# One load of five weight rows issued as five strided loads, and two small loads issued by ScalarE, in a gated attention decode step

## The chip, the cores and the metric

The kernel runs on one core of a Trainium2 chip. A core has five engines, each with its own instruction stream: TensorE (PE) multiplies matrices, VectorE (DVE) and GpSimd (POOL) do elementwise work and reductions, ScalarE (ACT) does activations and copies, and SyncE (SP) mostly issues DMAs. Sixteen DMA engines move data between the chip's main memory (HBM) and the core's on-chip memory (SBUF), which has 128 partitions. The metric is the time of one execution on the device, in microseconds (us).

## The reference

The step mixes one token's attention over a cache with a feed-forward layer, by a gate:

```
def _A_ref(x, k_cache, v_cache, wq, wo):          # B=2, Sq=1, D=640, H=32, Sk=4096, Dh=128
    q = (x @ wq).reshape(B, Sq, H, Dh).transpose(0, 2, 1, 3)
    scores = einsum("bhqd,bhkd->bhqk", q, k_cache) * (Dh ** -0.5)
    o = einsum("bhqk,bhkd->bhqd", softmax(scores), v_cache)
    return o.transpose(0, 2, 1, 3).reshape(B, Sq, H * Dh) @ wo
def _B_ref(x, w1, w2):                            # w1: 640 x 1728, w2: 1728 x 640
    return silu(x @ w1) @ w2
g = sigmoid((x * gate_w).sum(-1, keepdims=True))
return g * _A_ref(...) + (1 - g) * _B_ref(...)
```

Everything is float32. The two caches hold 134 MB each, the weights some 30 MB, and each byte of them is used once.

## The kernel before

SBUF holds three slabs of 64 KB per partition, `v`, `b` and `a` (`slabs`). The work runs through stages:

- **Start.** SP loads w1 into slab `a`, then x and the gate vector into the small tile `xs` (4 to 8 partitions of 640 bytes each), then w2 and wq. `xs` is cleared by POOL first (line 332), so x waits for that clear. DVE transposes `xs` (line 449), takes gate products (lines 453 to 460) and multiplies w1 by x (lines 472 and 475); PE finishes the feed-forward part (lines 487 and 567) and makes the queries (line 642). ACT's first instruction loads an activation table; its first work is the gate's exponential (line 506).
- **Sixteen items**, each a group of four heads for one of the two batch entries. For an item a K slab of 8.4 MB and a V slab of 8.4 MB are loaded. POOL and DVE multiply K by the query (lines 707 and 713), DVE sums and finds the peak (lines 723 to 741), ACT takes exponentials (line 752), PE multiplies by V (line 799), and DVE and PE fold the result into the columns `oP` (lines 821 to 871). K alternates between slabs `a` and `b`, V uses `v` and at the last item `a`.
- **End.** The 4096 rows of wo come in four groups (`load_wo`): two of them as one load of 5.1 MB and one as a load of 2.6 MB, into slab `v`, and the last one into slab `b`, cut in three: five of the eight rows that a partition holds (12,800 bytes in each of 128 partitions), then two rows (5,120 bytes), then one (2,560 bytes). PE multiplies the first three groups at line 590 (`in_halves`), ACT copies the sum at line 602, PE folds it at line 607 (`merge`), and the last group is multiplied at line 620 (`in_quarters`), which waits for the five rows, then for the two, then for the one. DVE copies the result (line 929) and SP stores it.

Every load is issued by SP, in program order, from one line (72, `Flow.dma`). `Flow` records operations with what they read and write; `plan` gives each its waits on semaphores. A load counts its own semaphore up by 16 when all of it has landed. The loads of wo are issued as soon as the last K slab and the last but one V slab have been used, and queue behind the last V load. A load of 128 partitions is served by all sixteen DMA engines; each engine has its own queue of the packets that are its share.

```
        cuts = (0, PD) if g < NP - 1 else (0, FIRST * D, PD - D, PD)
        after = f.users(part(n)) if g == NP - 1 else v_users
        for k, (c0, c1) in enumerate(zip(cuts, cuts[1:])):
            f.dma("SP", slab[n][:, at + c0 : at + c1], src[:, c0:c1], writes=part(n, g % (NP - 1) + k), after=after)
```

Of the kernel before, what the change touches and what calls it, by code (L numbers as in the profile page):

```python
# [189 lines left out]
def gated_decode(nc, x, kc, vc, wq, wo, w1, w2, gate, out):  # L190
    P = 128
# [4 lines left out]
    Q = 4  # L196
# [10 lines left out]
    HB = 16  # L207
# [4 lines left out]
    NP = HQ // 2  # L212
# [8 lines left out]
    f = Flow(nc)  # L221
    V, S_, T_, G_ = nc.vector, nc.scalar, nc.tensor, nc.gpsimd

    def sb(name, shape, align=32):
        return nc.alloc_sbuf_tensor(name, shape, F32, align_bytes=align)[tuple([slice(None)] * len(shape))]
# [7 lines left out]
    slab = {n: slabs[:, k * SLAB : (k + 1) * SLAB] for k, n in enumerate("vba")}  # L233

    def part(n, *ks):
        return [f"{n}.{k}" for k in (ks or range(8))]
# [13 lines left out]
    g = sb("g", [P, NP * B])  # L250
# [19 lines left out]
    oP, xs = oP_xs[:, : -D // Q], oP_xs[:, -D // Q :]  # L270
# [5 lines left out]
    oT = ps_m[:64, 256:512].rearrange("p (n r) -> p n r", r=32)  # L276
    early, acc = ps_acc[:, :W2], ps_0[:, :W]

    h_e, h_v, h_o, *h_k = (f.sem(n) for n in ("weights", "values", "rows", "even", "odd"))


# [32 lines left out]
    def load_wo(g):  # L314

        n, at = ("v", g * PD) if g < NP - 1 else ("b", 0)
        if g == 0:
            src = wo[: 2 * PR * P, :].rearrange("(g p n) d -> p g (n d)", g=2, n=PR)
            to = slab["v"][:, : 2 * PD].rearrange("p (g c) -> p g c", g=2)
            f.dma("SP", to, src, writes=part("v", 0, 1), after=v_users)  # L320
            return
        if g == 1:
            return
        src = wo[g * PR * P : (g + 1) * PR * P, :].rearrange("(p n) d -> p (n d)", n=PR)
        cuts = (0, PD) if g < NP - 1 else (0, FIRST * D, PD - D, PD)
        after = f.users(part(n)) if g == NP - 1 else v_users
        for k, (c0, c1) in enumerate(zip(cuts, cuts[1:])):
            f.dma("SP", slab[n][:, at + c0 : at + c1], src[:, c0:c1], writes=part(n, g % (NP - 1) + k), after=after)

    f.op("POOL", lambda: G_.memset(oP_xs, 0.0), writes=["oP", "xs"])
    f.dma("SP", slab["a"][:, : J * F], w1.rearrange("(p j) f -> p (j f)", j=J), writes=part("a"))
    f.dma("SP", xs[0:P:HB, :], x.rearrange("b s (c n) -> (s c) b n", c=Q), reads=["xs"], writes=["xs0"])
    f.dma("SP", xs[HB // 2 : P : 32, :], gate.rearrange("(c n) -> c n", c=Q), reads=["xs"], writes=["xs1"])
    f.dma(
        "SP",
        slab["v"][:, : FH * HD],
# [1 line left out]
        writes=part("v", 0),  # L340
# [9 lines left out]
        reads=["ident"],  # L350
        writes=["ident"],
# [11 lines left out]
        reads=["ident"],  # L363
        writes=["block"],
# [6 lines left out]
        reads=["block"],  # L371
        writes=["fold"],
# [4 lines left out]
        reads=["ident"],  # L377
        writes=["sel"],
# [4 lines left out]
        reads=["ident"],  # L383
        writes=["half"],
# [9 lines left out]
        reads=["sel"],  # L394
        writes=["pick"],
# [4 lines left out]
        reads=["sel"],  # L400
        writes=["own"],
# [4 lines left out]
        reads=["ident"],  # L406
        writes=["side"],
# [6 lines left out]
        reads=["block"],  # L414
        writes=["spread"],
# [4 lines left out]
        reads=["ident"],  # L420
        writes=["mask"],
    )
    f.op("DVE", lambda: V.memset(join, 0.0), writes=["join"])
    for e in range(2):
        ends, at = join[:, e, ::HB], 64 + HB * (1 - e)
# [5 lines left out]
            reads=["ident", "join"],  # L431
            writes=["join"],
        )
        for t in (at, at + 32):
# [3 lines left out]
                reads=["ident", "join"],  # L438
                writes=["join"],
# [10 lines left out]
        reads=["xs0", "xs1"],  # L450
        writes=["xt"],
# [5 lines left out]
        reads=["xt"],  # L457
        writes=["gx"],
    )
    f.op("DVE", lambda: V.reduce_sum(gp, gx.rearrange("p j b -> p b j"), axis=AX.X), reads=["gx"], writes=["gp"])  # L460
    rows = ps_v
# [4 lines left out]
    for b in range(B):  # L466
        for j in range(J):
            at = xt[:, j, HB * b : HB * b + 1]
# [11 lines left out]
                reads=part("a") + ["xt"],  # L480
                writes=[f"hsum{b}"],
            )

    def mm_hr():
# [18 lines left out]
        reads=["ones", "gp"],  # L503
        writes=["ps_o"],
# [6 lines left out]
        reads=["ge"],  # L511
        writes=["g"],
# [4 lines left out]
        reads=["g"],  # L517
        writes=["gc"],
# [7 lines left out]
    for e in range(2):  # L526
# [3 lines left out]
            reads=["ps_v"],  # L530
            writes=[f"spaced{e}"],
# [8 lines left out]
        reads=["he", "gc"],  # L540
        writes=["he"],
    )
    for e in range(2):
# [5 lines left out]
            reads=["he", "turned", "half", "seq"],  # L549
            writes=[f"seq{e}"],  # L550
# [125 lines left out]
    for u in range(2):  # L676
        for b in range(B):
# [7 lines left out]
                reads=[f"ps_{u}", "mask"],  # L685
                writes=[f"qall{u}{b}"],
# [200 lines left out]
    for i in range(N + 1):  # L887
# [21 lines left out]
        if i == N - 1:  # L909
            v_users = f.users(part("v"))  # L910
            for g_ in range(NP):
                load_wo(g_)
# [45 lines left out]
    ops, at = f.ops["PE"], 0  # L958
    while at < len(ops):
# [7 lines left out]
        at = end  # L967
# [21 lines left out]
```

## Time and profile before

| | us |
|---|---|
| median of three runs | 696.17 (695.96 to 696.38) |
| the profiled execution's own time | 695.97 |
| its span, first to last instruction | 694.6 |

| engine | busy in the span, us | share |
|---|---|---|
| DVE | 506.9 | 73% |
| POOL | 265.6 | 38% |
| PE | 211.9 | 31% |
| ACT | 40.0 | 6% |

No compute engine is near full. The page of the profile cuts the span into 40 slices; in its row "DMA" a 9 says that the sixteen DMA engines were busy 90% of the slice or more. The same quantity can be asked for any stretch: a row of the table of windows gives the stretch and its length, then the busy time of each engine in it with the number of instructions, the granted TensorE clock, the mean busy share of the DMA engines, and the rate in GB/s. A packet is counted in the window in which it starts, so that short windows are grainy. In the timeline a row gives start, duration, engine, line, operation, output and inputs, and in brackets how long the engine had been idle and what ended that; "SPq" is SP's sequencer issuing a DMA. A row of the DMA issues gives the number of loads, the size of one, and the time from issue to landing.

### The profile page before, as it was taken

How to read it: one execution, taken by the hardware profiler on the slowest of the kernel's cores; microseconds unless marked ns; L12 is line 12 of the kernel's file. 1: busy time of each engine (PE TensorE's matmuls, PEld its weight loads, DVE VectorE, ACT ScalarE, POOL GpSimd, SP SyncE). 2: the span in 40 equal slices, each digit the busy share in tenths (PEclk: the TensorE clock that was granted, in tenths of full speed). 3: DMA queues.
4: the chain of work that ended last, by engine and by line, in shares of the span. 5: the costliest groups of instructions: out<-in, count | busy, mean ns of one | idle time of the engine just before them, and what ended most of it. 6: DMA issues, size and time to landing. Idle time of an engine off the chain costs nothing. (4 is left out here: it accounts for less than half of the span.)

```text
span 694.6 us, 3767 instructions
## 1 busy us (share of the span) xinstructions
PE 211.9 (31%) x1440; PEld 70.2 (10%) x1440; DVE 506.9 (73%) x269; ACT 40.0 (6%) x152; POOL 265.6 (38%) x26
## 2 busy tenths in 40 slices
PE   0073033151331506060412305060513215060556
PEld 0031010010110101010100101010101001010112
DVE  3910958898989697886959596986959595977901
ACT  0001010101010101010010101010000101010100
POOL 1000908190827090815335180906244270907100
PEclk9997556565565657566575757575665757575779
DMA  9999999999999999999999999999999999999997
GB/s 383 429 426 473 426 423 427 423 464 434 423 430 423 442 457 423 423 430 434 464 423 423 430 426 468 426 423 430 423 468 430 423 430 423 453 445 423 430 417 309
DMA packets 6051, 298.32 MB, mean 429 GB/s; under 512 B 652, under 2 KB 672, under 8 KB 928
## 3 DMA queue, kind: packets, MB, share of 16 engines
q1 hardware_dynamic: 6048, 298.27, 99.3%
q8 instruction: 3, 0.05, 0.0%
HBM read 298.26 MB, written 0.01 MB: 429 GB/s over the span
## 5 line engine op out<-in xcount | busy, mean ns | idle before, releaser
L707 POOL TENSOR_TENSOR slabs<-slabs,qsb 128x7680 f32<-128x7680 f32 x16 | 262.4, 16400 | 378.9 <-DMA slabs<-in_A_k_cache_dram 330.8
L723 DVE TENSOR_REDUCE s<-slabs 128x68 f32<-128x8704 f32 (+1 forms) x32 | 276.3, 8677 | 0.0
L799 PE MATMUL ps<-slabs,pz 128*32 128x512 f32 x1024 | 147.2, 739 | 337.1 <-PEq L156 328.9
L713 DVE TENSOR_TENSOR slabs<-slabs,ps 128x8704 f32<-128x8704 f32 x16 | 147.5, 9221 | 103.8 <-DMA slabs<-in_A_k_cache_dram 103.2
L799 PEld LDWEIGHTS ps<-slabs,pz 128*32 128x32 f32 x1024 | 39.7, 132 | 433.5 <-issue 425.2
L752 ACT ACTIVATE pz<-s,nb 32x128 f32<-32x128 f32 x64 | 25.5, 398 | 545.8 <-PE ps L799 353.2
L837 PE MATMUL ps<-osb,pick 128*128 128x512 f32 x32 | 21.1, 747 | 60.9 <-PEq L156 59.9
L821 DVE SCALAR_TENSOR_TENSOR osb<-ps,rg,own 128x512 f32<-128x512 f32 x16 | 12.0, 750 | 23.4 <-PE ps L799 23.1
L852 DVE TENSOR_REDUCE row<-ps 64x128 f32<-64x512 f32 x16 | 10.9, 682 | 24.0 <-PE ps L837 24.0
L773 PE MATMUL ps<-rs,fold 128*128 128x1 f32 x32 | 6.2, 262 | 40.9 <-PEq L156 40.8
L475 DVE SCALAR_TENSOR_TENSOR slabs<-slabs 128x1728 f32<-128x1728 f32 x8 | 16.2, 2019 | 0.3
L487 PE MATMUL ps<-slabs,xz_col 128*32 128x432 f32 x16 | 3.1, 927 | 33.4 <-DVE slabs L475 33.4
L837 PEld LDWEIGHTS ps<-osb,pick 128*128 128x128 f32 x32 | 5.4, 211 | 75.0 <-issue 73.1
L752 ACT ACTIVATION_READ_ACCUMULATOR pz<-s,nb 32x1 f32 x64 | 11.8, 184 | 0.0
L773 PEld LDWEIGHTS ps<-rs,fold 128*128 128x128 f32 x32 | 6.2, 226 | 54.2 <-issue 53.3
L859 DVE STREAM_TRANSPOSE ps<-row 64x256 f32<-64x256 f32 x16 | 10.3, 643 | 0.6
L567 PE MATMUL ps<-slabs,seq 128*32 128x320 f32 x54 | 9.2, 496 | 3.7 <-DVE seq L546 3.7
L642 PE MATMUL ps<-slabs,xz_col 128*32 128x512 f32 x80 | 9.8, 593 | 0.0
L652 PE MATMUL ps<-qall,spread 128*128 (+1 forms) x32 | 9.0, 371 | 0.8 <-ACT qall L680 0.8
L929 DVE COPY slabs<-ps 128x160 f32<-128x160 f32 x1 | 0.3, 324 | 11.9 <-PE ps L620 11.9
L590 PE MATMUL ps<-slabs,oP_xs 128*32 128x320 f32 x96 | 6.9, 434 | 2.4 <-DMA slabs<-in_A_wo_dram 2.4
L652 PEld LDWEIGHTS ps<-qall,spread 128*128 128x128 f32 x32 | 6.1, 236 | 1.7 <-ACT qall L680 1.7
(63 smaller groups left out, 69.8 us busy)
## 6 DMA issues: line engine op xcount, KB each, us to landing
slabs<-in_A_wq_dram SPq DMA_DIRECT2D x1, 10240.0 KB, 44.5
slabs<-in_B_w_dram SPq DMA_DIRECT2D x2, 4320.0 KB, 16.9
slabs<-in_A_wo_dram SPq DMA_DIRECT2D x1, 5120.0 KB, 22.7
slabs<-in_A_wo_dram SPq DMA_DIRECT2D x1, 2560.0 KB, 28.3
slabs<-in_A_wo_dram SPq DMA_DIRECT2D x1, 1600.0 KB, 31.9
slabs<-in_A_wo_dram SPq DMA_DIRECT2D x1, 640.0 KB, 32.9
slabs<-in_A_wo_dram SPq DMA_DIRECT2D x1, 320.0 KB, 33.2
slabs<-in_A_k_cache_dram SPq DMA_DIRECT2D x16, 47.9
```

Of the source, the lines that this page charges most:

```text
L475: lambda b=b, j=j, at=at: V.scalar_tensor_tensor(hsum[:, b, :], w1t[:, j, :], at, hsum[:, b, :], op0=ALU.mult, op1=ALU.add)
L652: return T_.matmul(ps_q[:, :DH], spread, qall.rearrange("p n b u d -> p (n b u) d")[:, i, :], start=True, stop=True,)
L707: lambda: G_.tensor_mul(k[:, CV:, :], k[:, CV:, :], qsb[:, None, :].to_broadcast([P, C - CV, DH])),
L713: lambda: V.tensor_mul(k[:, :CV, :], k[:, :CV, :], ps_q[:, None, :DH].to_broadcast([P, CV, DH])),
L723: lambda c0=c0, c1=c1: V.reduce_sum(Ss[i % 2][:, c0:c1], k[:, c0:c1, :], axis=AX.X),
L752: last = S_.activation(pz[lo:hi, :, 4 * q : 4 * q + 4], s[lo:hi].rearrange("p (g c) -> p g c", c=4), AF.Exp, bias=nb[lo:hi], scale=SCALE, ...
L773: lambda *_: T_.matmul(ps_t[:, :1], fold.rearrange("p a q c -> p (a q c)"), rs, start=True, stop=True),
L799: last = T_.matmul(ps_v[32 * q : 32 * q + 32, :], pz[:, gr, :], v[:, gr, :], start=(gr < 4), stop=(gr >= NG - 4),)
L821: lambda: V.scalar_tensor_tensor(osb, ps_v.rearrange("p (c d) -> p c d", d=DH), rg, own[:, :, None].to_broadcast([P, 4, DH]), op0=ALU.mult ...
L837: lambda *_: T_.matmul(ps_o, pick, osb.rearrange("p c d -> p (c d)"), start=True, stop=True),
L852: lambda: V.reduce_sum(row, ps_o[:64].rearrange("p (c d) -> p d c", d=DH), axis=AX.X),
L859: lambda: V.transpose(oT.rearrange("p n (e i) -> p n e i", e=2), twice),
```

## The change

The load of five rows of the last group of wo (slab `b`, 128 partitions) is replaced by five loads on SP into the same places: partitions 1, 5, 9, ... (32 of them), 2, 6, ... (32), 3, 7, ... (32), then 0, 4, ..., 92 (24) and 96, 100, ..., 124 (8). They share one semaphore, which counts to 16, 32, 48, 64 and 80; PE waits for 80. The loads of x and of the gate are issued by ACT, not by SP, with the same wait for POOL's clear of `xs`.

```
+    SPARED = 8 * 12
...
         for k, (c0, c1) in enumerate(zip(cuts, cuts[1:])):
-            f.dma("SP", slab[n][:, at + c0 : at + c1], src[:, c0:c1], writes=part(n, g % (NP - 1) + k), after=after)
+            to, rows, key = slab[n][:, at + c0 : at + c1], src[:, c0:c1], part(n, g % (NP - 1) + k)
+            if g < NP - 1 or k:
+                f.dma("SP", to, rows, writes=key, after=after)
+                continue
+            ranges = [slice(m, P, 4) for m in range(1, 4)] + [slice(0, SPARED, 4), slice(SPARED, P, 4)]
+            first = f.sem("five_rows")
+            for m, r in enumerate(ranges):
+                f.dma("SP", to[r], rows[r], writes=key if m == 4 else (), after=after, count=(first, 16 * m + 16))
...
-    f.dma("SP", xs[0:P:HB, :], x.rearrange("b s (c n) -> (s c) b n", c=Q), reads=["xs"], writes=["xs0"])
-    f.dma("SP", xs[HB // 2 : P : 32, :], gate.rearrange("(c n) -> c n", c=Q), reads=["xs"], writes=["xs1"])
+    f.dma("ACT", xs[0:P:HB, :], x.rearrange("b s (c n) -> (s c) b n", c=Q), reads=["xs"], writes=["xs0"])
+    f.dma("ACT", xs[HB // 2 : P : 32, :], gate.rearrange("(c n) -> c n", c=Q), reads=["xs"], writes=["xs1"])
```

At the end of the program SP's list of loads reads so before the change; a row has the line, the operation, the output and its source, and the shape (partitions by elements of a partition).

```order
30 L72 DMA slabs<-in_A_v_cache_dram 128x16384
31 L72 DMA slabs<-in_A_k_cache_dram 128x16384
32 L72 DMA slabs<-in_A_v_cache_dram 128x16384
33 L72 DMA slabs<-in_A_k_cache_dram 128x16384
34 L72 DMA slabs<-in_A_v_cache_dram 128x16384 x2
35 L72 DMA slabs<-in_A_wo_dram 128x2x5120
36 L72 DMA slabs<-in_A_wo_dram 128x5120
37 L72 DMA slabs<-in_A_wo_dram 128x3200
38 L72 DMA slabs<-in_A_wo_dram 128x1280
39 L72 DMA slabs<-in_A_wo_dram 128x640
40 L72 DMA out_dram<-slabs 4x2x160
```

The same place on SP after the change:

```order
31 L72 DMA slabs<-in_A_v_cache_dram 128x16384 x2
32 L72 DMA slabs<-in_A_wo_dram 128x2x5120
33 L72 DMA slabs<-in_A_wo_dram 128x5120
34 L72 DMA slabs<-in_A_wo_dram 32x3200 x3
35 L72 DMA slabs<-in_A_wo_dram 24x3200
36 L72 DMA slabs<-in_A_wo_dram 8x3200
37 L72 DMA slabs<-in_A_wo_dram 128x1280
38 L72 DMA slabs<-in_A_wo_dram 128x640
39 L72 DMA out_dram<-slabs 4x2x160
```

The row of 128 partitions by 3200 elements has become three rows of 32 partitions, one of 24 and one of 8; what stands ahead of it and behind it is the same.

ACT's list begins so after the change:

```order
0 L72 DMA oP_xs<-in_A_x_dram 8x1x160
1 L72 DMA oP_xs<-in_gate_w_dram 4x160
2 L514 ACT_TABLE_LOAD
3 L514 ACTIVATE ge<-ps 128x2
4 L542 ACTIVATE he<-turned 128x28
```

The two small loads stand ahead of the table load, which was ACT's first row (its line 506 is line 514 now, since eight lines were added above it); on SP they stood between the loads of w1 and w2, which now follow each other.

## The prediction
> **What bounds the kernel now.** I read the page's slices first, then the DMA queues.
>
> ```profile
> DMA  9999999999999999999999999999999999999997
> GB/s 383 429 426 473 426 423 427 423 464 434 423 430 423 442 457 423 423 430 434 464 423 423 430 426 468 426 423 430 423 468 430 423 430 423 453 445 423 430 417 309
> DMA packets 6051, 298.32 MB, mean 429 GB/s; under 512 B 652, under 2 KB 672, under 8 KB 928
> q1 hardware_dynamic: 6048, 298.27, 99.3%
> q8 instruction: 3, 0.05, 0.0%
> ```
>
> The reader is to see that the sixteen DMA engines are busy all the time: 99.3% of the span is spent on the program's own loads. 298.3 MB at 429 GB/s is 695 us, the whole span. Each engine moves 429 / 16 = 26.8 GB/s, and nothing in the change alters the number of bytes. So only two things can move the time: the beginning, before the stream runs, and the end, where it runs out. The chain of waits names the end:
>
> ```profile
> 657.78 31.89 DMA slabs<-in_A_wo_dram
> 689.67 0.14 issue
> 689.80 2.16 PE ps L620 x56
> 691.97 0.02 issue
> 691.99 0.51 PE ps L620 x8
> 692.50 0.02 issue
> 692.52 0.32 DVE slabs L929
> ```
>
> The five rows land at 689.67, PE multiplies, and its last 8 matmuls start at 691.99. The timeline says what held PE there:
>
> ```profile
> 691.23 0.41 PEld L620 LDWEIGHTS ps<-slabs,oP_xs 128*17 128x17 f32 x16 [0.20 <-DMA slabs<-in_A_wo_dram]
> 691.99 0.13 PEld L620 LDWEIGHTS ps<-slabs,oP_xs 128*17 128x17 f32 x8 [0.36 <-DMA slabs<-in_A_wo_dram]
> ```
>
> Both times a load of wo: PE is waiting at the end, not late. So what counts is when the last packet of the last row comes. Windows over that stretch show it (in a row, the last two numbers are the DMA engines' mean share and GB/s):
>
> ```profile
> 684.00:689.50 5.50, 2.97 (x44) 1.07 (x40) 0.00 (x0) 0.42 (x1) 0.00 (x0) 1.00 0.97 405
> 689.50:690.25 0.75, 0.45 (x16) 0.46 (x20) 0.00 (x0) 0.00 (x0) 0.00 (x0) 1.00 0.78 311
> 690.25:691.50 1.25, 1.25 (x43) 1.01 (x36) 0.00 (x0) 0.00 (x0) 0.00 (x0) 1.00 0.18 74
> 691.50:692.50 1.00, 0.93 (x24) 0.25 (x12) 0.00 (x0) 0.00 (x0) 0.00 (x0) 1.00 0.00 0
> ```
>
> Up to 689.5 nearly all engines work; by 690.25 most have run out; then for another 1.25 us there is a rate of 74 GB/s, which is 74 / 26.8 = 2.8 engines. About **three of sixteen engines** finish 1.25 us after the other thirteen, and PE's end hangs on them. The page offers a cause, three packets of instructions: 0.05 MB in three is about 16 KB each, 0.6 us of an engine at 26.8 GB/s, and an engine whose queue never runs dry never makes up for such a delay. That there are three of each fits; that they are the same is inferred.
>
> **The change part by part.** *The five rows.* A partition's share is 5 x 640 x 4 = 12.8 KB, 0.478 us of an engine. A load of 128 partitions gives each of 16 engines 8 such shares. The three loads of 32 partitions give 2 to each, as before. I take it that a load is dealt in equal shares to as many of the 16 engines, counted from the first, as divide it: 24 partitions then go two each to 12 engines, and 8 go one each to 8. Eight engines have 9 shares, four have 8, and the last four have 6. No load of 24 or 8 such rows stands in this trace, so the effect has two ends: nothing moves (all dealt evenly), or 25.6 KB less on four engines and 12.8 KB more on eight. I take the second, since 24 can't be split evenly over 16.
>
> If the three late engines are among the four, they end at 691.50 - 0.96 = 690.54; the eight that got more end at 690.25 + 0.48 = 690.73. The later one counts: 691.50 - 690.73 = **0.77 us gained**. The five rows' own landing moves likewise, so PE, with 0.20 and 0.36 us of waiting in hand, moves as a whole.
>
> [...]
>
> *Issuing five loads.*
>
> ```profile
> slabs<-in_A_wo_dram SPq DMA_DIRECT2D x1, 1600.0 KB, 31.9
> slabs<-in_A_wo_dram SPq DMA_DIRECT2D x1, 640.0 KB, 32.9
> slabs<-in_A_wo_dram SPq DMA_DIRECT2D x1, 320.0 KB, 33.2
> 656.84 2.31 SPq L72 DMA_DIRECT2D slabs<-in_A_wo_dram  x5
> 1.85 0.71 SPq L72 DMA_DIRECT2D oP_xs<-in_A_x_dram  x1
> 2.61 0.54 SPq L72 DMA_DIRECT2D oP_xs<-in_gate_w_dram  x1
> ```
>
> SP issued five loads of wo in 2.31 us, 0.46 each; four more cost 1.8 us, or 2.8 at the 0.71 of x, the dearest load of few partitions. Behind them on SP stand the loads of two rows and of one, and the store at the end. They land 32.9 and 33.2 us after their issue, so 2.8 us is hidden ten times over: 0.
>
> Whether the engines lose time between short loads: five loads issued 0.46 apart landed 31.9, 32.9 and 33.2 us after issue, which is 0.46 + 1.0 = 1.5 us and 0.8 us apart; the bytes need 655 KB / 429 = 1.53 us and 0.76. No gap is seen between one queued load and the next, so I take 0 for four more; the upper end is the 0.04 that the rounding of those rows leaves, four times, 0.2.
>
> [...]
>
> *x and the gate on ACT.*
>
> ```profile
> 0.74 0.39 SPq L72 DMA_DIRECT2D slabs<-in_B_w_dram  x1
> 0.73 1.28 ACT L506 ACT_TABLE_LOAD   x1 [0.73 <-PEq L979]
> 3.67 0.44 SPq L72 DMA_DIRECT2D slabs<-in_A_wq_dram  x1
> 13.88 0.46 DVE L449 STREAM_TRANSPOSE slabs<-oP_xs 128x160 f32<-128x160 f32 x1 [7.85 <-DMA oP_xs<-in_gate_w_dram]
> 14.74 1.11 DVE L472 TENSOR_SCALAR slabs<-slabs 128x1728 f32<-128x1728 f32 x1
> 33.34 0.34 SPq L72 DMA_DIRECT2D slabs<-in_A_k_cache_dram  x1
> slabs<-in_A_wq_dram SPq DMA_DIRECT2D x1, 10240.0 KB, 44.5
> 37.04 0.17 ACT L506 ACTIVATE ge<-ps 128x2 f32<-128x2 f32 x1 [35.02 <-PE ps L502]
> ```
>
> On SP they stood between w1 and w2, 1.25 us of issue and a wait for POOL. w2 and wq are issued some 2 us earlier without them, but w1, issued at 0.74, still keeps the engines busy until about 13.7, just ahead of DVE's start at 13.88: nothing runs dry that now doesn't. On ACT's own queue x no longer stands behind w1's packets; DVE's transpose and gate work can be done by then, and line 472 may start at 13.8, not 14.74. That 0.9 us ends where the first K load is issued, 33.34, while wq keeps the engines fed until 3.67 + 44.5 = 48.2: 15 us of cover, worth 0. On ACT the table load stands behind the two loads and their wait, some 3 us; its first user runs at 37.04. Also 0. Without these covers the costs would be 0.9 gained and 3 lost.
>
> Sum: 695.97, the profiled execution's own time (694.6 of span and 1.4 around it), less 0.77 is 695.2. That execution lies 0.2 under the median of the runs, so I predict **695.4** on the scale of the median 696.17.
>
> **The rivals.**
>
> *R1, a late engine is not among the four.* Nothing in the profile numbers the engines; the windows sum over them. If the latest is one of the eight, it ends 0.48 us later: 696.65. If it is one of the four that keep 8 shares, or if the loads are dealt evenly after all (the change doesn't do what it says), nothing happens: 696.2. Against R1: runtime traffic of one kind, three packets on three engines, is more likely to sit on neighbouring engines than scattered, and a neighbouring three is spared together or missed together; missing is as possible as not.
>
> *R2, engines collide on the way into SBUF (slower).* [...] At half the rate the eight engines' 9 shares take 8.6 instead of 4.3 us, and the end goes to 690.25 + 0.48 + 4.3 = 695.0, 3.5 us after before: 699.7. It decides from the moment it eats the 0.77 us gained, a fifth of the load's 3.8 us; past 0.2% of the whole, 1.4 us, from 2.2 us. Some overlap of phases makes 698 to 699 likelier than 699.7. Against it: taken together, every fourth partition covers the same range as 128 do.
>
> [...]
>
> *R3, faster by more than expected.* At best the 93 KB after 690.25 would be spread over all engines, 0.2 us, a gain near 1.05: 695.1. More than 1.4 would need the beginning to shorten as well, by the 0.9 at line 472, against its 15 us of cover.
>
> **How the numbers follow.** A measurement tells about 0.2%, 1.4 us, from no change. Forecast 0.48 (694.9 to 695.9). R1 0.26 (695.9 to 696.9). R2 0.20, of which 0.18 beyond 1.4 us (697.6 to 699.7). R3 beyond 1.4 us 0.06. So faster 0.06, same 0.48 + 0.26 + 0.02 = 0.76, slower 0.18. The range goes from 694.8, below which only R3 lies, up into R2 to 698.0, which leaves out its dearer two thirds, 0.13, and R3's 0.06.
>
> **What would show each step.** Windows after 690: in the forecast the rate falls off once, between 690.0 and 690.8, without a tail of three engines, and the last matmuls of line 620 start near 691.2. With R1 the tail stays, at 691.5 or 692.0. With R2 the rate before 690 drops well under 405 GB/s. At the start DVE's line 449 should run near 6 instead of 13.88, once DVE is done with its tables, and line 472 near 13.8, with the first K load issued 0.9 earlier and everything from 48 on where it was. I am wrong on the mechanism if the tail vanishes and the time doesn't follow, or if the time falls before the stage of wo.

## The result, and the profile after

The change made the kernel slower by three microseconds.

| | median, us | lowest to highest | executions |
|---|---|---|---|
| before | 695.99 | 695.73 to 697.31 | 16 |
| after | 698.96 | 696.75 to 700.96 | 16 |

The ratio is 1.0037 with a 95% interval of 1.0027 to 1.0047 (this ratio, here and below, is not formed from the medians, which alone give 1.0043). Besides the median, the spread has grown: 1.6 us before, 4.2 after. The profiled execution took 696.75, which is the lowest of the sixteen, so the trace below shows 0.8 of the 3.0 us that the median lost. The rest has to be found by experiments.

The chain of waits of after ends so (start, duration, what):

```profile
661.01 29.54 DMA slabs<-in_A_wo_dram
690.55 0.14 issue
690.69 2.53 PE ps L628 x64
693.22 0.02 issue
693.24 0.32 DVE slabs L937
```

Line 628 is line 620 of before. The five rows land at 690.55, where they landed at 689.67, so 0.88 later; PE then runs its 64 matmuls without a pause, and DVE starts 0.72 later than before. The windows of after, with the four of the prediction (the last two numbers are the DMA engines' mean share and GB/s):

```profile
684.00:689.50 5.50, 2.88 (x44) 1.07 (x40) 0.00 (x0) 0.42 (x1) 0.00 (x0) 1.00 0.99 328
689.50:690.25 0.75, 0.00 (x0) 0.00 (x0) 0.00 (x0) 0.00 (x0) 0.00 (x0) 1.00 1.05 304
690.25:691.50 1.25, 0.81 (x24) 0.82 (x28) 0.00 (x0) 0.00 (x0) 0.00 (x0) 1.00 0.81 326
691.50:692.50 1.00, 1.00 (x40) 0.93 (x28) 0.00 (x0) 0.00 (x0) 0.00 (x0) 1.00 0.21 82
```

In the first row the share is 0.99 but the rate has fallen from 405 to 328 GB/s. All sixteen engines are busy, yet they move less: none is short of work, each packet takes longer. The packets themselves say so. A packet of 12.8 KB is a partition's share of the five rows; in before 127 of the 128 took 0.48 us, in after those that start from 686.7 on took 0.5 to 1.0. The bytes that were not moved by 689.50 (5.5 us at 77 GB/s less, 0.42 MB) are moved afterwards, at 326 GB/s, when before was nearly done.

At 691.50 to 692.50 the rate is 82 GB/s. That looks like the tail of before (74 GB/s at 690.25 to 691.50), one microsecond later, but it is not made by the same engines. The profile doesn't number the engines; their packets can still be strung together, since on one engine each packet starts as the one ahead of it ends (within 0.03 us). In before three engines end at 691.46 to 691.58, the other thirteen by 690.32. In after, strung so, eight engines carry nine packets of 12.8 KB, four carry eight and four carry six. The three late ones are among the four with six; they end at 691.69 to 691.82, and the last two of all, at 692.15 and 692.20, carry nine.

That the three engines are late because of the three packets of instructions, which the prediction inferred, can be seen in before. These packets start at 52.32, 110.27 and 684.48 and take some 0.96 us each. The sixteen engines finish the load that lands at 48 us within 0.6 us of each other; one is 1.2 us late in the load that lands near 68, two in the one that lands near 126, and three in the five rows.

The first microseconds of after, where x and the gate now stand on ACT (its sequencer is "ACTq"), and the first K load:

```profile
1.85 1.15 ACTq L72 DMA_DIRECT2D oP_xs<-in_A_x_dram  x1
3.03 0.53 ACTq L72 DMA_DIRECT2D oP_xs<-in_gate_w_dram  x1
3.59 1.28 ACT L514 ACT_TABLE_LOAD   x1 [3.59 <-POOL xz_col L361]
13.39 0.46 DVE L457 STREAM_TRANSPOSE slabs<-oP_xs 128x160 f32<-128x160 f32 x1 [7.37 <-DMA oP_xs<-in_gate_w_dram]
14.26 1.11 DVE L480 TENSOR_SCALAR slabs<-slabs 128x1728 f32<-128x1728 f32 x1
32.86 0.34 SPq L72 DMA_DIRECT2D slabs<-in_A_k_cache_dram  x1
```

DVE still waits for the gate until 13.39 (13.88 before), and the first K load is issued 0.48 us earlier, at 32.86.

### The profile page after: what moved, and what is told of

Read it like the earlier page. It is cut to its first block, busy times and chain, and to the rows that moved or that the text cites. A ratio compares the mean times of both kernels' runs of the same rounds, so it can differ in the third digit from the quotient of the medians.

```text
span 695.4 us, 3771 instructions
## 1 busy us (share of the span) xinstructions
PE 210.0 (30%) x1440; PEld 69.9 (10%) x1440; DVE 506.8 (73%) x269; ACT 40.0 (6%) x152; POOL 265.6 (38%) x26
## 5 line engine op out<-in xcount | busy, mean ns | idle before, releaser
L807 PE MATMUL ps<-slabs,pz 128*32 128x512 f32 x1024 | 145.6, 732 | 338.9 <-PEq L156 331.3
```

What stands on the lines that cost most here:

```text
L807: last = T_.matmul(ps_v[32 * q : 32 * q + 32, :], pz[:, gr, :], v[:, gr, :], start=(gr < 4), stop=(gr >= NG - 4),)
```

## The experiments

Two theories were set against each other and then beside each other. The one supposes that engines collide on the way into SBUF, and that the loads of fewer than 32 partitions are to blame (P in some expectations). The other says that the longer wait of PE lowers its granted clock (C). Their rivals in the expectations are X (the second DMA queue costs), N (the number of loads or the stride costs) and D (the late landing is the whole loss). In the diffs below, `ranges` is the list of partition slices from the diff of the change, whose loop over them comes with it; "before" and "after" name the kernel that was edited.

**The two edits apart.** First x and the gate alone, with the one load of five rows:

```
 # before
-    f.dma("SP", xs[0:P:HB, :], ...)
-    f.dma("SP", xs[HB // 2 : P : 32, :], ...)
+    f.dma("ACT", xs[0:P:HB, :], ...)
+    f.dma("ACT", xs[HB // 2 : P : 32, :], ...)
```

> The kernel before with only x and the gate issued by ScalarE. [...] If the second DMA queue is what costs (theory X), it is slower by 0.3 to 0.4% and its times spread over some 4 us like those of the changed kernel.

It took 696.03 (11 executions), ratio 1.0001 (0.9992 to 1.0010): the two loads cost and bring nothing. Then the five loads alone, with x and the gate on SP:

```
 # before
+            ranges = [slice(m, P, 4) for m in range(1, 4)] + [slice(0, 96, 4), slice(96, P, 4)]
```

> The kernel before with only the five strided loads; x and the gate stay on SyncE. Theory P: the whole loss is here, 0.2 to 0.5% slower with a wide spread, and the rate from 686.5 on falls under 330 GB/s. Theory X: within 0.1% of before.

It took 698.98 (698.03 to 700.74, 5 executions), ratio 1.0052 (1.0039 to 1.0066): the whole loss. Its profiled execution took 698.03, and its chain of waits differs from that of after in one row:

```profile
661.08 29.50 DMA slabs<-in_A_wo_dram
690.58 0.14 issue
690.72 3.82 PE ps L628 x64
694.54 0.02 issue
694.56 0.33 DVE slabs L937
```

The rows land at 690.58, as in after (690.55), but the same 64 matmuls take 3.82 us, not 2.53. That is 1.29 us, and the two executions, 698.03 and 696.75, lie 1.28 apart. The windows of this kernel tell why (the third number from the end is the granted clock):

```profile
686.50:689.50 3.00, 1.82 (x30) 0.52 (x20) 0.00 (x0) 0.43 (x1) 0.00 (x0) 1.00 1.03 277
689.50:690.25 0.75, 0.00 (x0) 0.00 (x0) 0.00 (x0) 0.00 (x0) 0.00 (x0) 0.99 0.98 263
690.25:691.50 1.25, 0.78 (x13) 0.60 (x17) 0.00 (x0) 0.00 (x0) 0.00 (x0) 0.50 0.85 340
691.50:692.50 1.00, 1.00 (x20) 0.76 (x16) 0.00 (x0) 0.00 (x0) 0.00 (x0) 0.50 0.24 92
```

From 690.25 on the clock stands at 0.50, where after had 1.00 throughout, and a microsecond holds 20 matmuls instead of 40. The page's count of packets also shows how the loads were dealt:

```profile
q1 hardware_dynamic: 6100, 298.27, 99.2%
```

Before had 6048. A load ends with one packet of 4 bytes on every engine that carries it, 16 of them for the one load of five rows (packets under 512 B: 652 in before, 704 in after). 52 more are 68 in its place: 16 for each of the three loads of 32, and 20, which is 12 and 8, for those of 24 and 8. So two things are lost: a late landing, and in some executions the clock of the last matmuls.

**Which property of the five loads.** Four loads of 32, every fourth partition, keep the stride and nearly the number:

```
 # before
+            ranges = [slice(m, P, 4) for m in range(4)]
```

> Four loads of 32 partitions, every fourth partition each, no class of 24 and 8. Theory P: the three such loads of the changed kernel ran at full rate, so this equals the kernel before within 0.1%, its tail of three late engines included. If the number of loads or the stride is what costs (theory N), it is slower by three quarters of the loss of the five loads, 0.2% or more.

It took 696.08 (11 executions), ratio 1.0002 (0.9993 to 1.0011): neither four loads in place of one nor the stride costs anything. Four loads of 32 consecutive partitions keep the number and the size:

```
 # before
+            ranges = [slice(m, m + 32) for m in range(0, P, 32)]
```

> Four loads of 32 consecutive partitions each. [...] Theory N: the same as with every fourth partition.

It took 703.66 (703.23 to 704.50, 4 executions), ratio 1.0112 (1.0096 to 1.0127): a loss of 7.6 us, where N had the same as with every fourth partition. The two kernels' windows show what only the choice of partitions does. Every fourth partition:

```profile
684.00:686.50 2.50, 0.99 (x18) 0.42 (x17) 0.00 (x0) 0.00 (x0) 0.00 (x0) 1.00 0.98 407
686.50:689.50 3.00, 1.99 (x32) 0.65 (x24) 0.00 (x0) 0.43 (x1) 0.00 (x0) 1.00 0.95 398
690.25:691.50 1.25, 1.25 (x43) 0.93 (x36) 0.00 (x0) 0.00 (x0) 0.00 (x0) 1.00 0.20 78
```

Blocks of 32:

```profile
684.00:686.50 2.50, 0.01 (x2) 0.00 (x0) 0.00 (x0) 0.00 (x0) 0.00 (x0) 1.00 1.01 197
686.50:689.50 3.00, 2.08 (x32) 0.94 (x32) 0.00 (x0) 0.00 (x0) 0.00 (x0) 1.00 1.02 218
692.50:693.50 1.00, 0.00 (x0) 0.00 (x0) 0.00 (x0) 0.00 (x0) 0.00 (x0) 0.54 0.99 230
```

With all engines busy (share 1.0) the rate is 197 to 230 GB/s, half of the mean 429. The bytes are the same and so is the number of packets (6096 in both), only the partitions that are loaded together differ. What is scarce is not shown: the rows of wo that are read together in main memory change with the partitions too, and no run keeps the one and changes the other; that it is the way into SBUF is the author's guess. The chain of waits with blocks of 32 shows where the loss lies:

```profile
659.29 35.92 DMA slabs<-in_A_wo_dram
695.21 0.14 issue
695.34 4.38 PE ps L628 x64
```

The rows land 5.5 us later than before (695.21 against 689.67), and the matmuls, at a clock that has fallen by 693, take 4.38 instead of 2.70 us from first to last, 1.7 more.

The class of 32 that the change cuts into 24 and 8 was then cut into four loads of 8 (partitions 0 to 28, 32 to 60, 64 to 92, 96 to 124, every fourth):

```
 # before
+            ranges = [slice(m, P, 4) for m in range(1, 4)] + [slice(m, m + 32, 4) for m in range(0, P, 32)]
```

> Three loads of 32 partitions as in the change, the fourth class as four loads of 8 (partitions 0 to 28, 32 to 60, 64 to 92, 96 to 124, every fourth): eight engines carry 10 shares of 12.8 KB, the other eight 6. If only the engines' shares count, late engines among the second eight end 0.96 us earlier and the time falls by up to 0.3 us or stays. [...]

It took 698.03 (696.73 to 699.93, 10 executions), ratio 1.0026 (1.0017 to 1.0035). An eleventh, the profiled one, ran at a mean granted clock of 0.55 (0.66 to 0.67 in the others) and took 708.76; its trace says nothing of the tail, so the kernel was profiled once more:

> The four loads of 8 partitions once more, for an undisturbed profile (the first one ran at a granted clock of 0.55). [...]

This one took 697.95, and its windows read:

```profile
684.00:686.50 2.50, 0.99 (x20) 0.45 (x20) 0.00 (x0) 0.00 (x0) 0.00 (x0) 1.00 0.96 399
686.50:689.50 3.00, 1.96 (x32) 0.62 (x24) 0.00 (x0) 0.42 (x1) 0.00 (x0) 1.00 1.04 329
```

The row before 686.50, in which the loads of 32 run, is at the full 399 GB/s. The next has 329 with a share of 1.04, between the 398 of four loads of 32 and the 277 of 24 and 8. Both ways of cutting the fourth class into fewer than 32 partitions that were tried slow the engines, to 329 GB/s and to 271 to 277. In this trace the late engines are again among those with the fewest shares, and the engines with ten end last, near 692.35.

No run here shows which engine wrote which partition, and why these loads slow the engines is not shown either.

**The clock.** If the clock falls because PE stands idle, PE must be slower even where the rows land on time. Here six of the eight rows of the group ahead are not multiplied:

```
 # before, in in_halves
-        for k in range(PR):
+        for k in range(PR) if g < NP - 2 else range(PR - 2, PR):
```

> The kernel before, its loads untouched; six of the eight rows of the third group of wo are left out of the product (24 of 32 matmul pairs less at line 590, so the output is not the reference's). Theory C: TensorE is busy for less than 1.5 us in the 3.4 us ahead of the five rows' landing at 689.7, the clock is at half for the last group, and the kernel with less work is slower, 696.8 to 698.0. Theory D: the end hangs on the landing alone, 696.0 as before.

With less work it took 697.89 (697.12 to 698.11, 10 executions), ratio 1.0024 (1.0015 to 1.0034). Its timeline on PE:

```profile
685.62 0.75 PE L590 MATMUL ps<-slabs,oP_xs 128*32 128x320 f32 x8 [1.51 <-DMA slabs<-in_A_wo_dram]
686.92 0.47 PE L607 MATMUL ps<-slabs,join 128*17 128x160 f32 x8 [0.55 <-ACT slabs L602]
689.71 4.47 PE L620 MATMUL ps<-slabs,oP_xs 128*17 128x160 f32 x64 [2.33 <-DMA slabs<-in_A_wo_dram]
```

PE works 0.75 and 0.47 us in what is now a long wait. The windows of the same kernel:

```profile
682.40:685.80 3.40, 1.89 (x32) 0.73 (x28) 0.00 (x0) 0.00 (x0) 0.00 (x0) 1.00 0.97 411
685.80:689.20 3.40, 1.04 (x16) 0.13 (x8) 0.00 (x0) 0.43 (x1) 0.00 (x0) 0.82 0.95 398
689.20:692.60 3.40, 2.89 (x45) 2.15 (x49) 0.00 (x0) 0.00 (x0) 0.00 (x0) 0.50 0.34 136
```

The rows land as early as before and the rate is before's, but the last 64 matmuls take 4.47 instead of 2.65 us. 1.8 us, at a clock of 0.50, is the whole loss of 1.9: with less work ahead of the last matmuls the clock fell, and 1.8 is the full price here. PE did not stand idle all the while: from 685.80 to 689.20 it was busy for 1.04 of 3.40 us.

The clock of the traces moves in steps: between two changes in the trace of before lie, for example, 3.41, 6.83, 10.24, 17.07 or 23.89 us, all multiples of 3.41, and the changes come at other moments in each execution (the last to 1.00 at 671.75 in before, at 672.74 in after). So PE's work is counted here in the step which ends at a possible change:

| execution | step, us from the start | PE's matmuls in it, us | clock after it |
|---|---|---|---|
| before | 685.40 to 688.81 | 2.63 | 1.00 |
| after | 686.39 to 689.80 | 1.99 | 1.00 |
| the five loads alone | 686.83 to 690.24 | 1.49 | 0.50 |
| before with less work | 684.55 to 687.96 | 1.21 | 0.50 |

In the traces of before and after, 111 steps of 3.41 us are at full clock: the 35 of them that hold 1.65 us of matmuls or less were followed by half clock, the 76 that hold 1.84 or more by full clock. After and the five loads alone had nearly the same wait (1.76 and 1.85 us): their steps fell differently.

The counterpart is the changed kernel with three matmuls of no use in the wait:

```
 # after, ahead of in_quarters
+    f.op(
+        "PE",
+        lambda: [
+            T_.matmul(ps_q[:, :256], ident, qall.rearrange("p n b u d -> p (n b u d)")[:, :256], start=True, stop=True)
+            for _ in range(3)
+        ][-1],
+        reads=["ident", "qall00"],
+        writes=["ps_q"],
+    )
```

> The changed kernel with three extra matmuls (128 columns by 256, into a bank that nothing reads any more) between the fold at line 615 and the last group, so that TensorE isn't idle while it waits for the five rows. Theory C (besides the late landing, the wait lets the granted TensorE clock fall to half in many runs, and the last 64 matmuls pay for it): the clock stays at 1.0 to the end, the median falls from 699.0 to about 696.8 and the spread from 4 us to under 1.5. Theory D (the whole loss is the landing of the rows): nothing changes, 699.0 with the same spread, or slower by part of the 1.3 us of extra matmuls.

It took 698.25 (696.48 to 698.98, 11 executions), ratio 1.0029 (1.0020 to 1.0038), where 696.8 had been expected. The fillers did what they were for: in the profiled execution (696.63) PE was busy in 686.50 to 690.25 and the clock stayed at 1.00. Its chain of waits has them at line 939, three matmuls in six passes:

```profile
689.01 1.49 PE ps L939 x6
690.50 0.10 issue
690.60 2.55 PE ps L628 x64
```

But only 0.7 us of the loss went, and 1.7 us of the spread (2.5 us is left); 2.2 us remained. So the clock is the smaller part, and the theory that all beyond the traced 0.8 us is clock has fallen. The 0.7 is no better than a rough size: the intervals of the two kernels overlap, and no trace shows that the fillers held the clock in the longer executions too. What remains must be shown without the clock. In the next pair the last group is cut from 64 matmuls to 24 (three rows of eight, one per load), so that a low clock has little to slow:

```
 # after, and before, in in_quarters
-        for k in range(PR):
+        for k in (0, FIRST, PR - 1):
```

> The changed kernel with five of the last group's eight rows left out of the product (24 matmuls at line 628 instead of 64, one row of each of the three loads; the output is not the reference's). TensorE waits for every load as before, but the clock costs it little: 24 matmuls at half clock are some 0.6 us longer. Beside the kernel before with the same cut: if the late landing makes the slow executions (theory D), this one is 2 to 3 us slower and its times spread over 3 us or more; if the clock makes them (theory C), it is 0.7 to 1.2 us slower with a spread under 1.5.

> The kernel before with the same five rows left out of the last group's product: the base for the run above. The last row's landing sets the end, so 695.5 to 696.1, as before, with a spread under 1.5 us.

After with the short tail took 698.35 (696.92 to 698.99, 6 executions); before with it took 696.17 (695.84 to 696.83, 11 executions). The difference is 2.2 us again, and the clock has little part in it: in before's trace the last eight matmuls ran at half clock, 0.74 us instead of 0.47. What PE waits for, in the timeline of after with the short tail:

```profile
690.99 0.47 PE L628 MATMUL ps<-slabs,oP_xs 128*17 128x160 f32 x8 [2.03 <-DMA slabs<-in_A_wo_dram]
692.18 0.47 PE L628 MATMUL ps<-slabs,oP_xs 128*17 128x160 f32 x8 [0.72 <-DMA slabs<-in_A_wo_dram]
692.93 0.47 PE L628 MATMUL ps<-slabs,oP_xs 128*17 128x160 f32 x8 [0.29 <-DMA slabs<-in_A_wo_dram]
```

And in that of before with the short tail:

```profile
689.63 0.47 PE L620 MATMUL ps<-slabs,oP_xs 128*17 128x160 f32 x8 [0.62 <-DMA slabs<-in_A_wo_dram]
691.06 0.47 PE L620 MATMUL ps<-slabs,oP_xs 128*17 128x160 f32 x8 [0.96 <-DMA slabs<-in_A_wo_dram]
691.84 0.74 PE L620 MATMUL ps<-slabs,oP_xs 128*17 128x160 f32 x8 [0.32 <-DMA slabs<-in_A_wo_dram]
```

All three landings are later, by 1.36, 1.12 and 1.09 us: not only the five rows, but the two and the one behind them. Again the profiled execution (696.92) is the lowest of its six.

The changed kernel itself was profiled once more, to have one of its longer executions in a trace:

> The changed kernel once more, for a profile of one of its slower executions (the profiled one took 696.75, the median is 698.96). Theory C: the granted clock is 0.5 in a part of the last 6 us, and the last 64 matmuls of line 628 take 3.5 us or more instead of 2.5. Theory D: clock 1.0, and the rows land 2 us later than in the first profile (690.55 for the five rows, 692.7 for the last).

The execution that was traced took 696.44, below all sixteen of the result, with the clock at 1.00 to the end and PE's last matmuls from 690.45.

## Why the prediction was wrong

**What bounds the kernel** was right: the end hangs on the last packets, and each change of the landing came out in the time.

**The sum of the five rows** is the step that failed. It priced a share of 12.8 KB at 0.478 us on whichever engine carries it, so that fewer shares on four engines would be 0.96 us won there and one more share on eight would be 0.48 lost, 0.77 gained in all. This holds only if an engine keeps its 26.8 GB/s however the load is cut. From 686.50 to 689.50 the sixteen engines moved 271 to 277 GB/s in the kernels with 24 and 8, that is 17 GB/s each, against 398 with four loads of 32. All else in this step came true: the shares were dealt as nine, eight and six, and the three late engines were among the four with six. But the engine that ends last in after took 5.5 us for its nine shares (684.16 to 689.63), where the sum had 9 x 0.478 = 4.3, and that alone is more than the 0.77 that was to be gained.

**The price** in the traced execution agrees with the rate. From before and from after:

```profile
686.50:689.50 3.00, 1.97 (x32) 0.62 (x24) 0.00 (x0) 0.42 (x1) 0.00 (x0) 1.00 0.95 399
686.50:689.50 3.00, 1.88 (x32) 0.54 (x23) 0.00 (x0) 0.42 (x1) 0.00 (x0) 1.00 1.01 271
```

3 us at 128 GB/s less are 0.38 MB, and these take 0.9 us at the mean of 429; the landing moved by 0.88. In the median the landing costs more, 2.2 us by two independent runs (698.25 with fillers against 696.01 for before beside it, 698.35 against 696.17 with the short tail). The rest of the 3.0, some 0.7 (698.96 less 698.25), is put down to the clock.

**R2 comes nearest to what the runs show**, a time longer by a lower rate, with two faults. It put the loss on every fourth partition, and four loads of that kind cost nothing (1.0002); the place is the two loads of fewer than 32. And the argument against it, that every fourth partition covers the same range as 128, was taken to hold for the 24 and the 8 too, which cover parts of it; hence a chance of only 0.20. Its price, "likelier 698 to 699", contains the median of 698.96, in part by chance: it had no term for the clock. Its half of the rate, from which it had 699.7, no run shows for the loads of 24 and 8: they ran at 271 to 277 GB/s where before had 399, and half (197 to 230) came only with blocks of 32. That engines collide is not shown either.

**The clock was not foreseen at all.** The prediction said that PE waits at the end and moves as a whole. It does not always: behind a wait of 1.85 us, where before had 0.80, the 64 matmuls began at a clock of 0.50 in the 698.03 execution of the five loads alone, which cost 1.3 us; the kernel with less work paid 1.8.

**Right** were the terms at nothing. Three more issues on SP and three more queued loads cost nothing (four loads of 32: 1.0002; the fourth was not run by itself). x and the gate on ACT are worth nothing (1.0001), for the reason given: wq's cover is longer than what is won at the start. Its details were off: line 457 did not run near 6 but at 13.39, and the first K load was 0.48 earlier, not 0.9. On ACT's queue the twenty small packets of x and the gate go out between the packets of w1, which take 1.28 us each on an engine, and are spread over 6.43 to 13.04.

**Open.** Why most executions land 2.2 us late when the traced ones of after land 0.6 to 1.4 late (690.31 to 690.55 against 689.67, and the first of the pair with the short tail). The author's guess is that the sixteen engines stand differently to each other when the 24-partition load begins; no trace of a longer execution was had. What it is that runs short with blocks of 32 (197 to 230 GB/s) and with 24 and 8 (271 to 277), the way into SBUF, the rows read in main memory or something else, is not shown. A version that relieves the late engines without loads of fewer than 32 partitions was not tried, and none of the kernels was faster than before.

## What to carry to other kernels

Giving a late DMA engine less to do by splitting a load over partitions can cost more than it gains: here pieces of 32 partitions, one in four, kept the rate (398 GB/s), pieces of 24 and 8 did not (271 to 277). Look for a stretch with the DMA share at 1.0 and the rate below that of its neighbours: there the packets take longer, and work is not lacking (here a share of 1.01 at 271 GB/s, behind 0.96 at 397). Where PE waits at the end, price a longer wait twice, once for itself and once for the matmuls behind it at half the clock (here 3.82 us in place of 2.53). And compare the profiled execution with the spread of the others before the trace is taken for the loss: here it showed 0.8 of 3.0 us.

## What the runs showed that was not expected

- Leaving out work made a kernel slower: 24 matmuls fewer, 1.9 us more, since the clock fell to 0.50 before the last 64.
- Equal bytes, loads of equal size and all engines busy, but 398 or 218 GB/s, by the choice of the partitions that are loaded together.
- Four loads of 8 partitions lose about half as much of the rate as 24 and 8 (329 GB/s, between 398 and 277) and two thirds as much time (2.0 of 3.0 us).
- The late engines were relieved as planned, and the kernel was slower all the same: after ends on engines that were not late before.
